# Attention and routed experts on one core: the third batch's table matmuls put behind the attention, the first slot's rows turned before the last value products, and conditional slots in groups of 4, 2 and 2

## The chip, the cores and the metric

The kernel runs on one core of a Trainium2 chip. The metric is the device time of one launch in microseconds (us). The profiled execution is a single launch with the hardware profiler on; its span is the time from its first to its last instruction.

## The reference

Four batches of 768 tokens with 8 heads of 64 are attended to in chunks of 32, each with 16 positions to its left, 8 to its right and 8 memory keys. The result, 3072 rows of 512, goes through a mixture of 8 experts of which each row takes one.

```python
for c in range(S // 32):
    k_full = concat(mem_k, k[c_start - 16 : c_end + 8])     # clipped to 0..S
    a = softmax(q_c @ k_full.T / sqrt(D))
    out[c] = a @ concat(mem_v, v[c_start - 16 : c_end + 8])
x = out.transpose(0, 2, 1, 3).reshape(3072, 512)
logits = x @ w_gate + modality_bias[modality_id]
e = argmax(logits); gate_w = softmax(logits)[e]
y[rows of e] = gate_w * (relu(x[rows of e] @ w1[e]) @ w2[e])
```

## The kernel before, in words

**Attention.** The work is cut into 32 units: 16 pairs of heads (four to a batch), each in two halves of the sequence. The main loop runs 34 times (`i` from 0 to 33, `n` is 32) and keeps three units in flight. For one unit `scores` (L356) makes the score products on TensorE, `exps_t` turns them (L374) and ScalarE takes their exponential (L376), `attend` makes the value products (L386), `normalize` divides on VectorE (L394 to L401) into a tile `xb`, and `trans_x` turns `xb` for the router (L409, copy L412) and, with the second half, stores it to `xd` in memory from GpSimd's queue (L414). In its last turns the loop finishes units 30 and 31, and the opening slot of the experts is begun.

**Routing.** After each batch a generator `route(b)` makes the logits (L546; ScalarE copies them in two halves, L549), turns them to token order (L556), finds each token's expert and rank on VectorE, makes one-hots of ranks and tokens (`l1`, L661, and `a1`, L663; for the third batch two of six tiles on GpSimd and the others on VectorE), and multiplies them in six matmuls (L671) to a table that says which token stands in which place. VectorE subtracts that into the table so far (L672). `pump` takes steps of the generator between pieces of the attention. A step that needs TensorE waits, "late" ones longer, until enough turns of the loop have passed; the table matmuls are such a late step. `B - 2` is the third batch, whose table comes in the last turns.

**Experts.** Tokens are gathered into slots of up to 256 rows of one expert. `gather` fetches a slot's rows from `xd` with two indirect DMAs on GpSimd's queue (L765) into the tiles `xg0` and `xg1`; the opening slot takes rows of the first batches alone, and its gather is issued in the turn `i` = 29. `trans(half)` turns them on TensorE (L804) and splits them into a high part (ScalarE, L780) and a low part (VectorE, L781). `load_w` loads an expert's weights on SyncE's queue (first weights L723 and L729, second L733), each into a `raw` tile; `conv` splits such a tile (ScalarE's cast L736; the rest on VectorE or GpSimd, L738). `mm1(f)` makes one eighth of the hidden layer in 12 matmuls (L822) with the relu on ScalarE (L823) and its low part on VectorE (L826); `mm2` makes the output (L832), which is scaled and scattered by an indirect DMA (L857).

**Slots.** After the opening slot and some fixed ones stand 8 short conditional slots (none is taken for these tokens; their branch line is L1131), two fixed slots, 8 conditional slots of the usual size (for these tokens four are taken; their branch line is L1137), and three last slots. Each group of conditions is nested: a slot's condition lies in the one before it, and all close together. An engine that finds a condition false jumps past the nested slots to a block that sets semaphores right for what was skipped, waits there for its own earlier work, and then branches behind the nest.

**What sets the order.** TensorE, SyncE and GpSimd run their instructions as written. ScalarE's and VectorE's are put in order by a scheduler from `i` = 26 on to the slots, and as written after that.

Of the kernel before, what the change touches and what calls it, by code (L numbers as in the profile page):

```python
# [21 lines left out]
B, H, S, D = 4, 8, 768, 64  # L22
# [33 lines left out]
def tile_chunk_attention_top1_moe(  # L56
# [39 lines left out]
    def bank():  # L96
        return ps.tile([P, 512], F32, name="tr", tag="tr", bufs=4)
# [210 lines left out]
    def regroup_q(u):  # L308
        q2 = q2s.pop(u)
        qr = qrs[u] = wk.tile([P, 6, 2, D], F32, name="qr", bufs=1)  # L310
        nc.vector.tensor_copy(
            qr.rearrange("p x h d -> p h x d"), q2.rearrange("p h (x d) -> p h x d", d=D)
        )
# [36 lines left out]
    def scores(u, hf):  # L350
        kbd, qT = kbds[u % 2], qTs[u]
        sc = scs[u, hf] = ps.tile([P, 512], F32, name="sc", tag="sc", bufs=2)
        for t in range(3):
            for j in range(4):
                c = 4 * (3 * hf + t) + j
                nc.tensor.matmul(  # L356
                    sc[32 * j:32 * j + 32, t * P:(t + 1) * P], qT[:, 32 * c:32 * c + 32],
                    kbd[:, c].rearrange("p h m -> p (h m)"), start=True, stop=True,
                )
# [9 lines left out]
    def exps_t(u, hf):  # L369

        sb = sbs.pop((u, hf)).rearrange("p a m -> p (a m)")
        t = bank()
        for i in range(3):
            nc.tensor.transpose(t[:, i * P:(i + 1) * P], sb[:, i * P:(i + 1) * P], ident)  # L374
        PT = PTs[u, hf] = wk.tile([P, 3 * P], F32, name="PT")
        nc.scalar.activation(PT, t[:, 0:384], AF.Exp, scale=scale)  # L376
# [14 lines left out]
    def normalize(u, hf):  # L391
        av = avs.pop((u, hf))[:, 0:3 * W].rearrange("p (t w) -> p t w", t=3)
        den = sm.tile([P, 3, 2, 1], F32, name="den")
        nc.vector.tensor_scalar(den[:, :, :, 0], av[:, :, 2 * D:W], 1e-9, None, op0=ALU.add)  # L394
        pump(1)
        nc.vector.reciprocal(den, den)
        pump(1)
        if hf == 0:
            xbs[u] = wk.tile([P, NT, P], F32, name="xb", bufs=3)
        dst = xbs[u].rearrange("p t (h d) -> p t h d", d=D)[:, 3 * hf:3 * hf + 3]  # L400
        nc.vector.tensor_mul(  # L401
            dst, av[:, :, 0:2 * D].rearrange("p t (h d) -> p t h d", h=2), den.to_broadcast([P, 3, 2, D]))

    def trans_x(u, hf):
        b, g = divmod(u, 4)
        xb = xbs[u]
        t = bank()
        for i in range(3):
            nc.tensor.transpose(t[:, i * P:(i + 1) * P], xb[:, 3 * hf + i, :], ident)  # L409
        if hf == 0:  # L410
            xTs[u] = rt.tile([P, S], F32, name="xT", bufs=5)
        nc.scalar.copy(xTs[u][:, 384 * hf:384 * hf + 384], t[:, 0:384])  # L412
        if hf == 1:
            nc.gpsimd.dma_start(xd[b * S:(b + 1) * S, g * P:(g + 1) * P].rearrange("(t p) c -> p t c", p=P), xb)  # L414


    routing, now = [], [0]

    def pump(k, pe=False):
        k *= KB if routing and routing[0][2] == B - 2 else 1  # L420
        while k > 0 and routing:
            g, wait, b, since = routing[0]
            if wait:
                if not pe or now[0] < since + (wait == "late" or b < B - 2) + (wait == "late" and b < B - 2):
                    return
                pe = False
            r = next(g, None)
            if r is None:
                routing.pop(0)
                return  # L430
            routing[0] = (g, r if r != "v" else "", b, now[0])
            k -= r == "v"
# [346 lines left out]
    def split(x, sl, cols):  # L779
        nc.scalar.copy(xth[:, sl, cols], x)  # L780
        nc.vector.tensor_sub(xtl[:, sl, cols], x, xth[:, sl, cols].bitcast(F32))  # L781
# [17 lines left out]
    def trans(half):  # L799
        t = bank().rearrange("p (c n) -> p c n", c=2)  # L800
        for cc in range(2):
            for tt in range(2):
                c = 2 * half + cc
                nc.tensor.transpose(t[:, cc, tt * P:(tt + 1) * P], xg[tt][:, c * P:(c + 1) * P], ident)  # L804
        split(t, slice(2 * half, 2 * half + 2), slice(0, 256))
# [8 lines left out]
    def mm1(f, rest=False, whole=True):  # L814
        w = 256 + (NR if rest else 0)
        pw = bank()[:, 0:w]
        ph = pw[:, 0:256]

        for n in range(12):
            wt, x, c = ((wh, xth), (wl, xth), (wh, xtl))[n // 4] + (n % 4,)  # L820
            i, j = (f, c) if whole else (f - f % 4 + c, f % 4)
            nc.tensor.matmul(pw, wt[i][:, j * P:(j + 1) * P], x[:, c, 0:w], start=(n == 0), stop=(n == 11))  # L822
        nc.scalar.activation(hh[:, f], ph, AF.Relu)  # L823
        if rest:
            nc.scalar.activation(hq[:, f], pw[:, 256:], AF.Relu)
        nc.vector.scalar_tensor_tensor(hl[:, f], ph, 0.0, hh[:, f].bitcast(F32), op0=ALU.max, op1=ALU.subtract)  # L826
# [88 lines left out]
    units = [(u, hf) for u in range(NU) for hf in range(2)]  # L915
    n = len(units)
    for i in range(n + 2):
        live = i < n
        u, hf = units[i] if live else (NU, i % 2)
        now[0] = i  # L920
        if i == MAN:
            man.close()
        if live and i < n - 1:
            scores(u, hf)
        if 1 <= i <= n:
            exps_t(*units[i - 1])
        if live:
            less_max(u, hf)
            pump(1)
        if u + 1 < NU and hf == 0:  # L930
            trans_k(u + 1)
            regroup_q(u + 1)
            pump(3)
            store_k(u + 1, 1, 0, nc.scalar.copy)
            store_k(u + 1, 0, 0, nc.scalar.copy)
            store_k(u + 1, 0, 1, nc.scalar.copy)
            store_k(u + 1, 1, 1, nc.scalar.copy)
            pump(3)
        elif u + 1 < NU:
            share_v(u + 1)  # L940
            if u + 2 < NU:
                mem_keys(u + 2, nc.gpsimd)
            trans_q(u + 1)
            store_q(u + 1, 0)
            store_q(u + 1, 1)
            pump(5)
        elif live:
            pump(5)
        if 2 <= i < n:
            trans_x(*units[i - 2])  # L950
        if i == n - 2:
            scores(*units[i + 1])
        if 1 <= i <= n:
            attend(*units[i - 1])
        if i == n:
            trans_x(*units[i - 2])
            trans(0)
            trans(1)
            conv(4)
            conv(5, nc.gpsimd)  # L960
            normalize(*units[i - 1])
            mm1(0)
        if i > n:
            mm1(1)
        if i > n:
            trans_x(*units[i - 2])
        if 1 <= i < n:
            normalize(*units[i - 1])
            pump(1)
        if i >= 2:  # L970
            u2, hf2 = units[i - 2]
            if hf2 == 1 and u2 % 4 == 3:
                routing.append((route(u2 // 4), True, u2 // 4, 0))
        if i == 1:
            routing.append((more_constants(), False, -1, 0))
        if i == 6:
            assert not routing
            bias_rows()
        if i < n:
            pump(1, True)  # L980
        if live and hf == 0:
            if 0 < u < NU - 3:
                load_qk(u + 3)
            if u >= 1 and u - 1 + NVW < NU:
                load_v(u - 1 + NVW)
            if u == NU - 3:
                load_w(0, 0)
        if (u, hf) == (NU - 2, 1):
            c_ld.close()
            xp = ctx.enter_context(tc.tile_pool(name="xp", bufs=1, side="right"))  # L990
            ix = xp.tile([P, 2], I32, name="ix")
            gx = xp.tile([P, 2], I32, name="gx")
            xg = [xp.tile([P, XW], F32, name=f"xg{t}", align_bytes=256) for t in range(2)]
            xth, xtl = [xp.tile([P, 4, 256 + NR], F32R, name=f"xt{i}") for i in range(2)]
            hh, hl = [xp.tile([P, 8, 256], F32R, name=f"h{i}") for i in range(2)]
            gather(0)
        elif u == NU - 1:
            conv(2 * hf)
            conv(2 * hf + 1, nc.gpsimd)
# [117 lines left out]
    more = ExitStack()  # L1117
# [14 lines left out]
    slot(ROW_R1, rest=0, rest_next=1)  # L1132
    slot(ROW_X, rest=1)
    for i in range(NEXTRA):
        more.enter_context(tc.If(nextra > i))
        slot(ROW_X + i + 1)
    more.close()  # L1137
# [32 lines left out]
```

## Time and profile before

| what | us |
|---|---|
| median of three runs | 445.32 |
| lowest and highest of them | 441.22, 449.06 |
| the profiled execution | 444.95 |
| span of the profiled execution | 442.9 |

The profiled execution's mean granted TensorE clock is 0.98 of full speed. In a timeline each row is a run of equal instructions: when it begins, how long it lasts, engine, source line, operation, result and operands by the program's names, the count, and in brackets the engine's idle time just before with what ended it. PE is TensorE, PEld its weight loads, DVE VectorE, ACT ScalarE, POOL GpSimd, SP SyncE; a small q marks an engine's instruction queue.

### The profile page before, as it was taken

How to read it: one execution, taken by the hardware profiler on the slowest of the kernel's cores; microseconds unless marked ns; L12 is line 12 of the kernel's file. 1: busy time of each engine (PE TensorE's matmuls, PEld its weight loads, DVE VectorE, ACT ScalarE, POOL GpSimd, SP SyncE). 2: the span in 40 equal slices, each digit the busy share in tenths (PEclk: the TensorE clock that was granted, in tenths of full speed). 3: DMA queues.
4: the chain of work that ended last, by engine and by line, in shares of the span. 5: the costliest groups of instructions: out<-in, count | busy, mean ns of one | idle time of the engine just before them, and what ended most of it. 6: DMA issues, size and time to landing. Idle time of an engine off the chain costs nothing. (4 is left out here: it accounts for less than half of the span.)

```text
span 442.9 us, 11892 instructions
## 1 busy us (share of the span) xinstructions
PE 416.2 (94%) x4053; PEld 356.6 (80%) x4053; DVE 309.7 (70%) x754; ACT 268.9 (61%) x537; POOL 204.6 (46%) x409
## 2 busy tenths in 40 slices
PE   7799999998978988999999999999999989999993
PEld 4677787877756968989798998989898969898982
DVE  7878697798687899848366356868686864959530
ACT  6857878786738555647366355656565654756521
POOL 7998879798496932450144205313131035020101
PEclk9989999999999998999999999999999998999998
DMA  6879988898756210487096967414795206140101
GB/s 200 218 195 276 253 211 242 224 246 214 187 139 220 83 34 22 123 268 189 28 274 210 202 218 262 123 73 123 154 262 223 72 15 204 33 142 1 48 1 48
DMA packets 78309, 69.33 MB, mean 157 GB/s; under 512 B 36763, under 2 KB 64563, under 8 KB 78228
## 3 DMA queue, kind: packets, MB, share of 16 engines
q1 hardware_dynamic: 71488, 48.84, 40.8%
q0 software_dynamic: 5888, 19.41, 14.2%
q8 instruction: 37, 0.61, 0.6%
q14 instruction: 44, 0.36, 0.3%
q10 hardware_dynamic: 852, 0.11, 0.2%
HBM read 81.25 MB, written 16.58 MB: 221 GB/s over the span
## 5 line engine op out<-in xcount | busy, mean ns | idle before, releaser
L822 PEld LDWEIGHTS tr<-xt,w 128*128 128x128 f32 x1152 | 142.3, 191 | 6.7 <-issue 4.0
L822 PE MATMUL tr<-xt,w 128*128 128x256 f32 (+1 forms) x1152 | 143.7, 286 | 3.9 <-issue 2.6
L832 PE MATMUL av<-wh,h 128*128 128x512 f32 x384 | 125.7, 399 | 0.0
L826 DVE SCALAR_TENSOR_TENSOR h<-tr,h 128x256 fp32r<-128x256 f32 x96 | 40.6, 424 | 66.2 <-ACT h L823 47.8
L832 PEld LDWEIGHTS av<-wh,h 128*128 128x128 f32 x384 | 72.4, 189 | 16.5 <-issue 0.4
L832 PE MATMUL av<-wl,h 128*128 128x512 f32 x192 | 75.8, 395 | 0.0
L823 ACT ACTIVATE h<-tr 128x256 fp32r<-128x256 f32 x96 | 36.7, 384 | 55.3 <-PE tr L822 45.6
L738 DVE TENSOR_TENSOR wl<-raw,wh 128x512 fp32r<-128x512 f32 x91 | 63.4, 698 | 8.7 <-ACT wh L736 1.6
L857 POOL DMA_INDIRECT out_dram<-o,ix x24 | 24.4, 1018 | 95.0 <-ACT o L853 92.8
L306 POOL COPY vw<-vw 24x384 f32<-24x384 f32 (+1 forms) x128 | 59.7, 504 | 10.0 <-DMA vw<-in_v_dram 8.5
L738 DVE TENSOR_TENSOR w<-raw,w 128x512 fp32r<-128x512 f32 x93 | 60.0, 685 | 5.1 <-ACT w L736 2.5
L736 ACT CAST wh<-raw 128x512 fp32r<-128x512 f32 x96 | 58.7, 615 | 0.0
L736 ACT CAST w<-raw 128x512 fp32r<-128x512 f32 x96 | 53.0, 621 | 0.1
L348 ACT COPY kbd<-tr 64x672 f32<-64x672 f32 x62 | 48.2, 777 | 4.6 <-PE tr L342 3.5
L832 PEld LDWEIGHTS av<-wl,h 128*128 128x128 f32 x192 | 36.3, 189 | 7.8
L853 ACT ACTIVATE o<-av,gate 128x512 f32<-128x512 f32 x24 | 16.3, 689 | 39.5 <-PE av L832 31.1
L765 POOL DMA_INDIRECT xg<-xd,gx x24 | 27.2, 1133 | 17.5 <-POOL gx L763 4.9
L376 ACT ACTIVATE PT<-tr 128x384 f32<-128x384 f32 x32 | 15.8, 493 | 29.5 <-PE tr L374 29.3
L386 PE MATMUL av<-vw,PT 128*32 128x130 f32 x768 | 29.4, 287 | 1.4 <-ACT PT L376 1.4
L356 PE MATMUL sc<-kbd,qT 128*32 128x128 f32 x768 | 27.6, 277 | 1.5 <-DVE kbd L348 1.3
L386 PEld LDWEIGHTS av<-vw,PT 128*32 128x32 f32 x768 | 20.2, 113 | 7.5 <-issue 3.8
L356 PEld LDWEIGHTS sc<-kbd,qT 128*32 128x32 f32 x768 | 20.7, 111 | 5.1 <-issue 3.4
(253 smaller groups left out, 519.1 us busy)
## 6 DMA issues: line engine op xcount, KB each, us to landing
raw<-in_moe_w_dram SPq DMA_DIRECT2D x192, 256.0 KB
k<-in_k_dram SPq DMA_DIRECT2D x16, 384.0 KB
q<-in_q_dram SPq DMA_DIRECT2D x16, 384.0 KB
xd<-xb POOLq DMA_DIRECT2D x16, 384.0 KB, 4.8
vw<-in_v_dram SPq DMA_DIRECT2D x32, 184.0 KB
xs<-xg SPq DMA_DIRECT2D x14, 256.0 KB
xq<-xs SPq DMA_DIRECT2D x28, 128.0 KB
vw<-in_mem_v_dram SPq DMA_DIRECT2D x32, 48.0 KB
```

Source lines behind the costliest of these rows:

```text
L306: nc.gpsimd.tensor_copy(vw[r0:r0 + 24, c + 1:c + 1 + w, d], vw[r0 + 32:r0 + 56, c:c + w, d])
L348: copy(dst.rearrange("p c (i j) -> p c i j", j=2)[:, :, :, j], win)
L356: nc.tensor.matmul(sc[32 * j:32 * j + 32, t * P:(t + 1) * P], qT[:, 32 * c:32 * c + 32], kbd[:, c].rearrange("p h m -> p (h m)"), start=Tr ...
L386: nc.tensor.matmul(avb[32 * j:32 * j + 32, t * W:(t + 1) * W], PT[:, t * P + 32 * j:t * P + 32 * j + 32], vw[:, c, 0:W], start=True, stop= ...
L736: nc.scalar.copy(wh[i], raw[i])
L738: (eng or nc.vector).tensor_sub(wl[i][:, s], raw[i][:, s], wh[i][:, s].bitcast(F32))
L765: nc.gpsimd.indirect_dma_start(out=xg[t], out_offset=None, in_=xd[0:rows], in_offset=bass.IndirectOffsetOnAxis(ap=at[:, t:t + 1], axis=0))
L822: nc.tensor.matmul(pw, wt[i][:, j * P:(j + 1) * P], x[:, c, 0:w], start=(n == 0), stop=(n == 11))
L823: nc.scalar.activation(hh[:, f], ph, AF.Relu)
L826: nc.vector.scalar_tensor_tensor(hl[:, f], ph, 0.0, hh[:, f].bitcast(F32), op0=ALU.max, op1=ALU.subtract)
L832: nc.tensor.matmul(pos[t], x, w[8 + f], start=(f == 0 and n == 0), stop=(f == 7 and n == 2))
L857: nc.gpsimd.indirect_dma_start(out=out, out_offset=bass.IndirectOffsetOnAxis(ap=to[:, t:t + 1], axis=0), in_=outs[t], in_offset=None, boun ...
```

## The change

Three edits. First, `pump` holds the late step of the third batch until the turn `i` = 32, where it is called for behind `mm1(0)`. Second, in that turn the gathered rows of the opening slot are turned first (`trans(0)`, `trans(1)`), then unit 30 (`trans_x`), and only then come the last value products (`attend`) and their normalization; in the turn after it `trans_x` stands ahead of `mm1(1)`. Third, the 8 conditional slots are closed behind the fourth and the sixth, so that they make three nests of 4, 2 and 2.

```diff
         if wait:
-            if not pe or now[0] < since + (wait == "late" or b < B - 2) + (wait == "late" and b < B - 2):
+            if not pe or (wait == "late" and b == B - 2 and now[0] < n) or now[0] < since + (wait == "late" or b < B - 2) + (wait == "late" and b < B - 2):
                 return
...
+        if i == n:
+            trans(0)
+            trans(1)
+            trans_x(*units[i - 2])
         if i == n - 2:
             scores(*units[i + 1])
         if 1 <= i <= n:
             attend(*units[i - 1])
         if i == n:
-            trans_x(*units[i - 2])
-            trans(0)
-            trans(1)
+            normalize(*units[i - 1])
             conv(4)
             conv(5, nc.gpsimd)
-            normalize(*units[i - 1])
             mm1(0)
-        if i > n:
-            mm1(1)
+            pump(99, True)
         if i > n:
             trans_x(*units[i - 2])
+            mm1(1)
...
     for i in range(NEXTRA):
+        if i in (4, 6):
+            more.close()
         more.enter_context(tc.If(nextra > i))
         slot(ROW_X + i + 1)
     more.close()
```

TensorE at the end of the attention, as the kernel before has it (the value products of unit 29 stand first; `tr` and `av` are results, `xg` the gathered rows, `xt` their split halves, `a1` and `l1` the one-hots):

```order
L386 MATMUL av_2781<-vw2_128,PT_2756 32x130 x12
L671 MATMUL tr_2798<-a1_2677,l1_2676 128x192
L671 MATMUL tr_2798<-a1_2681,l1_2680 128x192
L671 MATMUL tr_2798<-a1_2685,l1_2684 128x192
L671 MATMUL tr_2798<-a1_2689,l1_2688 128x192
L671 MATMUL tr_2798<-a1_2693,l1_2692 128x192
L671 MATMUL tr_2798<-a1_2697,l1_2696 128x192
L374 MATMUL tr_2816<-ident_144,sb_2760 128x128 x3
L409 MATMUL tr_2826<-ident_144,xb_2722 128x128 x3
L386 MATMUL av_2832<-vw0_126,PT_2820 32x130 x12
L374 MATMUL tr_2857<-ident_144,sb_2824 128x128 x3
L386 MATMUL av_2863<-vw0_126,PT_2861 32x130 x12
```

And the same stretch in the changed kernel, to the first of the gathered rows:

```order
L386 MATMUL av_2781<-vw2_128,PT_2756 32x130 x12
L374 MATMUL tr_2805<-ident_144,sb_2760 128x128 x3
L409 MATMUL tr_2815<-ident_144,xb_2722 128x128 x3
L386 MATMUL av_2821<-vw0_126,PT_2809 32x130 x12
L374 MATMUL tr_2846<-ident_144,sb_2813 128x128 x3
L804 MATMUL tr_2852<-ident_144,xg0_2731 128x128
L804 MATMUL tr_2852<-ident_144,xg1_2732 128x128
```

The six table matmuls are gone from here (they stand behind `mm1(0)` now), and the eight transposes of the gathered rows, which in the kernel before come behind the last value products and the turning of unit 30, stand ahead of both.

ScalarE's list around the two logit copies (L549), from the cast of the first of the second weights on, before:

```order
L736 CAST wh8_2952<-raw8_2951 128x512
L823 ACTIVATE h0_2735<-tr_2922 128x256
L736 CAST wh9_2955<-raw9_2954 128x512
L412 COPY xT_2880<-tr_2937 128x384
L549 COPY lgs_3003<-tr_3004 128x384
L736 CAST wh10_2958<-raw10_2957 128x512
L549 COPY lgs_3003<-tr_3010 128x384
L736 CAST wh11_2961<-raw11_2960 128x512
L736 CAST wh12_2964<-raw12_2963 128x512
```

And in the changed kernel:

```order
L736 CAST wh8_2952<-raw8_2951 128x512
L736 CAST wh9_2955<-raw9_2954 128x512
L412 COPY xT_2870<-tr_2922 128x384
L736 CAST wh10_2958<-raw10_2957 128x512
L736 CAST wh11_2961<-raw11_2960 128x512
L823 ACTIVATE h0_2735<-tr_2928 128x256
L736 CAST wh12_2964<-raw12_2963 128x512
L549 COPY lgs_3003<-tr_3004 128x384
L549 COPY lgs_3003<-tr_3010 128x384
```

Three more casts stand ahead of the first logit copy, and two more ahead of the second.

TensorE between the fourth and the fifth conditional slot, before:

```order
L832 MATMUL av<-wh_2973,h_2735 128x512
L832 MATMUL av<-wl_2974,h_2735 128x512
L832 MATMUL av<-wh_2973,h_2736 128x512
L1137 COMPARE_AND_BRANCH
L822 MATMUL tr<-xt_2733,w_192 128x256 x4
L822 MATMUL tr<-xt_2733,w_193 128x256 x4
L822 MATMUL tr<-xt_2734,w_192 128x256 x4
```

And in the changed kernel:

```order
L832 MATMUL av<-wh_2973,h_2735 128x512
L832 MATMUL av<-wl_2974,h_2735 128x512
L832 MATMUL av<-wh_2973,h_2736 128x512
L1137 UNCONDITIONAL_BRANCH x5
L1137 COMPARE_AND_BRANCH
L822 MATMUL tr<-xt_2733,w_192 128x256 x4
L822 MATMUL tr<-xt_2733,w_193 128x256 x4
L822 MATMUL tr<-xt_2734,w_192 128x256 x4
```

The compare stands where it stood; the branches of the first nest's end are new ahead of it, and the same with three branches stands behind the sixth slot. In the kernel before all nine branches of the nest stand behind the eighth slot.

## Rows read from the trace of the kernel before

**Rows 1.** The page, part 1: busy time, share of the span, instructions.

```profile
PE 416.2 (94%) x4053; PEld 356.6 (80%) x4053; DVE 309.7 (70%) x754; ACT 268.9 (61%) x537; POOL 204.6 (46%) x409
```

**Rows 2.** TensorE's timeline, 124 to 146 us (start, us, engine, line, operation).

```profile
127.75 0.36 PE L671 MATMUL tr<-a,l 128*128 128x192 f32 x1 [0.51 <-POOL a L663]
129.32 0.47 PE L671 MATMUL tr<-a,l 128*128 128x192 f32 x2 [1.22 <-POOL a L663]
130.23 1.32 PE L671 MATMUL tr<-a,l 128*128 128x192 f32 x3 [0.43 <-DVE a L663]
...
135.66 0.87 PE L386 MATMUL av<-vw,PT 128*32 128x130 f32 x24 [0.64 <-ACT PT L376]
136.47 0.55 PE L409 MATMUL tr<-ident,xb 128*128 128x128 f32 x3
136.85 1.07 PE L804 MATMUL tr<-ident,xg 128*128 128x128 f32 x8
138.59 3.33 PE L822 MATMUL tr<-xt,w 128*128 128x256 f32 x24 [0.67 <-ACT xt L780]
...
142.17 1.94 PE L546 MATMUL tr<-xT,wg 128*32 128x384 f32 x16
...
145.57 0.60 PE L556 MATMUL tr<-ident,lgs 128*128 128x128 f32 x4
```

**Rows 3.** GpSimd's timeline, 125 to 146 us.

```profile
128.27 1.00 POOL L663 TENSOR_SCALAR a<-iota,ac,tokm 128x192 fp32r<-128x192 f32 x1
...
130.42 1.18 POOL L765 DMA_INDIRECT xg<-xd,gx  x1 [0.30 <-issue]
131.90 0.98 POOL L765 DMA_INDIRECT xg<-xd,gx  x1 [0.30 <-issue]
```

**Rows 4.** The tile xg, 129 to 138 us (durations in ns; DMA landings).

```profile
L804 PE MATMUL tr<-ident,xg x8: 272/273/304, 136.8 to 137.6; 128*128 128x128 f32 x8
...
DMA to landing us min/median/max: 3.6/4.3/5.0
```

**Rows 5.** TensorE's timeline behind the first nest and behind the second.

```profile
220.05 1.17 PE L822 MATMUL tr<-xt,w 128*128 128x288 f32 x7 [0.66 <-PEq L1131]
...
363.35 0.40 PE L832 MATMUL av<-wh,h 128*128 128x512 f32 x1
366.33 2.04 PE L822 MATMUL tr<-xt,w 128*128 128x256 f32 x11 [2.58 <-issue]
```

**Rows 6.** Branch line L1137, whole span, then from 363.9 us (ns, min/median/max).

```profile
L1137 PEldq COMPARE_BRANCH  x6: 65/74/3446, 269.9 to 363.9; - x6
...
L1137 PEldq EVENT_SEMAPHORE  x1: 51/51/51, 363.8 to 363.8; - x1
...
L1137 PEldq COMPARE_BRANCH  x1: 2218/2218/2218, 363.9 to 363.9; - x1
```

**Rows 7.** TensorE's timeline, 157.5 to 169 us.

```profile
157.82 0.81 PE L671 MATMUL tr<-a,l 128*128 128x192 f32 x6
158.46 0.42 PE L832 MATMUL av<-wh,h 128*128 128x512 f32 x1
...
166.37 0.30 PE L804 MATMUL tr<-ident,xg 128*128 128x128 f32 x1 [2.17 <-DMA xg<-xd,gx]
```

**Rows 8.** Windows: us, busy PE, PEld, DVE, ACT, POOL, clock, DMA, GB/s.

```profile
131.60:135.00 3.40, 3.40 (x33) 2.15 (x31) 1.03 (x4) 1.49 (x3) 0.98 (x1) 0.50 0.70 193
135.00:138.40 3.40, 2.28 (x36) 1.77 (x35) 2.28 (x6) 2.87 (x6) 2.20 (x5) 1.00 0.14 29
```

**Rows 9.** Branch line L1131, whole span (ns, min/median/max).

```profile
L1131 PEldq COMPARE_BRANCH  x1: 3667/3667/3667, 216.1 to 216.1; - x1
```

**Rows 10.** SyncE's timeline, 134 to 142 us.

```profile
136.80 4.27 SPq L733 DMA_DIRECT2D raw<-in_moe_w_dram  x8
```

**Rows 11.** ScalarE's timeline, 141 to 146 us.

```profile
141.34 0.62 ACT L736 CAST wh<-raw 128x512 fp32r<-128x512 f32 x1
...
144.15 0.48 ACT L549 COPY lgs<-tr 128x384 f32<-128x384 f32 x1
```

## The prediction

> **What bounds the kernel now.** I read the page's busy shares first: TensorE is busy for 94% of the span, no other engine for more than 70% [rows 1]. A cut in the work of another engine is then worth nothing unless TensorE waits for it, and the change removes no matmul: it can only move waits of TensorE. So the next view was TensorE's timeline at the two places that the diff touches, and there the brackets, which name what ended each idle time.
>
> At the attention's end TensorE waits three times for one-hots of the third batch's table (0.51, 1.22 and 0.43 us), once for the exponentials of the last unit (0.64) and once for the first slot's turned rows (0.67): 3.47 us in all before the logits of the last batch begin at 142.17 [rows 2]. The POOL timeline tells why the one-hots are late: the last of them that POOL makes ends at 129.27, and behind it in the same queue stand a store and the two halves of the first slot's gather [rows 3]. The gathered rows take 3.6 to 5.0 us from issue to landing [rows 4].
>
> At the conditional slots, which for these tokens are taken four times of eight, TensorE stands 2.58 us between the last matmul of the fourth and the first of the slot behind the nest [rows 5]. The rows of the branch line there show one taken jump of 3446 ns that ended under matmuls still queued, the wait for the engine's own work at 363.8, and behind it a second jump of 2218 ns [rows 6].
>
> **The table held back.** It removes the waits of 0.51, 1.22 and 0.43 us [rows 2]: behind mm1(0) the one-hots have been ready for long. No matmul goes; the six take 0.64 us by their spacing in the fourth batch's table, which runs at the full clock [rows 7]. The table's own readers plan slots behind the opening one, so the 10 us of delay has cover: the next gather that TensorE waits for is the one before 166.37, and it hangs on the fourth batch's table, from 157.82 on [rows 7]. Its order stays as it was, so what shifts the head shifts it as much.
>
> **The rows turned earlier.** The transposes of the gathered rows now stand ahead of the last value products. Nothing in the change moves the gather: POOL's order is the same, and the one-hots that hold its queue are still made there. Its halves are issued at 130.42 and 131.90 [rows 3], so the second lands between 135.5 and 136.9 by the two ends of [rows 4]; I take the middle, 136.2. In before the transposes start at 136.85 without a wait, because TensorE comes that late [rows 2]. In after it is there at about 130 (three waits gone, some 2 us of value products and transposes put behind), and stands idle for some 6 us. The wait for the gather takes the place of the four that go. One queue is held meanwhile: behind the waiting transposes stand the turning of unit 30, the last value products and mm1(0); DVE's last normalization, the last store to xd and SP's loads of the second weights wait for the value products in their turn.
>
> What follows the landing, by spacings in [rows 2]: seven of the eight transposes at 0.114 us each (the busy 1.07 less 0.27 for the one in flight, over seven; 0.27 from [rows 4]) 0.80; unit 30's transposes 0.38; the value products 0.81; mm1(0) 1.60 (from 138.59 to 142.17, less 0.38 of transposes, over two); the table 0.64; the last transposes 0.38; mm1(1) 1.60. Sum 6.2 us. The copies that mm1(0) waits for in before (0.67) now lie beside unit 30 and the value products, 1.2 us, so I cost that wait at nothing; uncovered it is 0.7 at most. The clock adds something: after the waits of before the profile shows 3.40 us at a granted 0.50, and then 1.00 [rows 8]. A longer idle time in after should bring such a stretch too; if it lies wholly in the work after the landing it costs half its length, 1.7 us, if in the idle time nothing. I take half, 0.9. Logits: 136.2 + 6.2 + 0.9 = 143.3, against 142.17: **+1.1 us**. Low end 135.5 + 6.2 = 141.7, -0.5; high end 136.9 + 6.2 + 1.7 = 144.8, +2.6. From the logits on TensorE's order is that of before.
>
> **The groups.** Eight nested conditions become 4, 2 and 2. With four slots taken, one jump over four slots becomes two jumps over two. The first is hidden as now by the queued matmuls. At its landing the engine waits for its own work, as now (363.8), and only then comes the second jump, with nothing left to hide it. Its price: the two forward jumps that the trace shows took 3446 ns [rows 6] and 3667 ns [rows 9]; the 2218 ns that stands there now goes. That is +1.23 to +1.45, and 0.1 for one compare more (65 to 74 ns where not taken [rows 6]). I take **+1.4 us**, nearest to both rows. [...] From above: 3.67 and a short jump of 2.2 behind it as now, +3.7. No trace of before shows a jump over two slots.
>
> [...] The row shows 3446 ns for a jump over four slots, some 1150 instructions on TensorE (144 matmuls with as many weight loads in each) [rows 6]. [...]
>
> **Sum.** 444.95 (the profiled execution; span 442.9) + 1.1 + 1.4 = 447.5 us. That execution lies 0.4 under the median of the three runs, 445.32, whose spread is 441.22 to 449.06, so no correction.
>
> **Rivals.**
> First, faster: the jump over two slots is short. Its place is the end of the nest, its price -1.9, and it decides as soon as the second jump takes under about 1.1 us (the 2.2 that goes, less the head's +1.1). 444.95 + 1.1 - 1.9 = 444.2; with the head's low end 442.6. For it: half the distance of any jump shown. Against it: 3446 and 3667 ns, and nothing shorter that was taken. Chance 0.25.
> Second, slower: the second weights, not TensorE, end the head. SP issues their loads at 136.80, 0.27 after the last value products [rows 2, 10]; in after these end at about 138.2 to 139.2, the loads start up to 2.6 later (139.4). ACT's list now has five casts of these weights ahead of both logit copies, where before it had two ahead of the first and a third ahead of the second. First cast 141.34 + 2.6 = 143.9 [rows 11]; then up to the second copy five casts at 0.57, a 0.37 copy, a relu of 0.28 and the first logit copy 0.37 (spacings, estimates): 147.8 in place of 144.15, +3.7, less 0.94 that the transposes at 145.57 have in hand today [rows 2, 11]: +2.7 in place of +1.1, 449.1 us. It decides from an ACT lag over 2.0 us. For it: the order; against it: the casts may catch up if loads land fast. Chance 0.18.
> Third, the waits simply vanish: 3.5 off the head, 1.4 on, 442.9. It needs the gather in by about 132; [rows 3, 4] exclude it unless POOL comes earlier. Chance 0.04. A remainder of 0.03 goes to a slower tail, both jumps and a fetch, 451.
>
> **How the numbers follow.** The forecast has 0.50, its own range 445.5 to 449.5. Sums of the ends: 442.6 (-0.5 and -1.9) and 451.3 (+2.6 and +3.7). The range 441.7 to 451.8 adds about 0.7 for the executions' own spread. Within 2% is 436.4 to 454.2, about what a measurement of this kernel can tell from no change: every case lies in it. Faster 0.02, same 0.95, slower 0.03.
>
> **What would show it.** Right: TensorE's first idle row of some 4 to 6 us stands at the gathered rows' transposes, released by the gather near 136; no idle time at the table; logits near 143.3; two jumps of 3.4 to 3.7 us on the branch line and about 4.0 us of idle time ahead of the first last slot. Wrong: the transposes start before 134, the second jump is under 1 us, or the logits' copies come after 147.

## The result and the profile after

The changed kernel takes 450.37 us (median of 10 runs, 448.25 to 451.93) against 444.84 for the kernel before (10 runs): 1.0134 times as long, 95% interval 1.0104 to 1.0163, or 6.0 us with 4.6 to 7.3. The forecast was slower by 2.5 us. Its outer range (441.7 to 451.8) held the time, the forecast's own range (445.5 to 449.5) did not, and both of its terms were about half of what the profiles show.

The profiled execution took 451.93 us with a span of 450.1. The page's first part answers to [rows 1]:

```profile
PE 416.2 (92%) x4053; PEld 357.6 (79%) x4053; DVE 306.8 (68%) x754; ACT 268.8 (60%) x537; POOL 201.8 (45%) x409
```

TensorE's busy time is the same to the tenth. By this page what came is idle time alone, as forecast; the question is which.

TensorE's timeline at the attention's end, which answers to [rows 2, 7]:

```profile
127.72 0.85 PE L386 MATMUL av<-vw,PT 128*32 128x130 f32 x24
...
130.16 0.52 PE L409 MATMUL tr<-ident,xb 128*128 128x128 f32 x3 [1.11 <-DVE xb L401]
...
135.47 0.45 PE L804 MATMUL tr<-ident,xg 128*128 128x128 f32 x1 [3.52 <-DMA xg<-xd,gx]
136.89 1.76 PE L804 MATMUL tr<-ident,xg 128*128 128x128 f32 x7 [0.97 <-DMA xg<-xd,gx]
...
139.21 1.52 PE L386 MATMUL av<-vw,PT 128*32 128x130 f32 x24
140.67 1.89 PE L822 MATMUL tr<-xt,w 128*128 128x256 f32 x12
142.40 0.81 PE L671 MATMUL tr<-a,l 128*128 128x192 f32 x6
...
144.88 1.50 PE L546 MATMUL tr<-xT,wg 128*32 128x384 f32 x16
...
150.53 0.93 PE L556 MATMUL tr<-ident,lgs 128*128 128x128 f32 x6 [2.52 <-ACT lgs L549]
...
172.38 0.98 PE L804 MATMUL tr<-ident,xg 128*128 128x128 f32 x7 [1.15 <-DMA xg<-xd,gx]
```

The waits at the table (L671) are gone, and in their place stand 1.11 us for VectorE's normalization of unit 29, 4.49 at the gathered rows and, further on, 2.52 at the logits' transposes. The times can't be set beside those of before as they stand: at 103 us, ahead of everything that the change touches, the two executions already differ by 1.36 us, and the value products of unit 29 (127.72 above) begin 1.33 later than in the kernel before:

```profile
126.39 0.85 PE L386 MATMUL av<-vw,PT 128*32 128x130 f32 x24
```

Counted from these products, the logits begin at 17.16 in place of 15.78 us (+1.4) and their transposes at 22.81 in place of 19.18 (+3.6). That is against one execution: five further profiles with the old head (e1, e7, e9, e13 and e14 below) have the logits at 15.7 to 16.9 and the transposes at 19.1 to 20.3, and against the mean of all six the shifts are 1.0 and 3.3.

GpSimd's timeline (answers to [rows 3]), then SyncE's [rows 10] and ScalarE's [rows 11]:

```profile
131.77 1.18 POOL L765 DMA_INDIRECT xg<-xd,gx  x1 [0.30 <-PE av L386]
133.25 0.98 POOL L765 DMA_INDIRECT xg<-xd,gx  x1 [0.30 <-issue]
```

```profile
141.00 4.51 SPq L733 DMA_DIRECT2D raw<-in_moe_w_dram  x8
```

```profile
146.31 0.62 ACT L736 CAST wh<-raw 128x512 fp32r<-128x512 f32 x1 [1.02 <-DMA raw<-in_moe_w_dram]
147.75 0.62 ACT L736 CAST wh<-raw 128x512 fp32r<-128x512 f32 x1 [0.83 <-DMA raw<-in_moe_w_dram]
...
149.49 0.62 ACT L736 CAST wh<-raw 128x512 fp32r<-128x512 f32 x1 [0.83 <-DMA raw<-in_moe_w_dram]
150.01 0.85 ACT L549 COPY lgs<-tr 128x384 f32<-128x384 f32 x2
```

The gather is issued where it was (1.35 later, the shift of the execution). The second weights' loads begin 4.20 later, 2.87 by the clock of the value products, and ScalarE then waits for them three times with both logit copies queued behind.

The clock at the head (windows; the clock is the third number from the right), which answers to [rows 8]:

```profile
132.00:135.50 3.50, 0.03 (x1) 0.06 (x1) 2.58 (x8) 1.13 (x3) 3.19 (x5) 0.83 0.81 209
135.47:139.00 3.53, 2.56 (x11) 2.15 (x11) 0.51 (x1) 1.13 (x3) 1.56 (x3) 0.50 0.51 168
139.00:141.00 2.00, 2.00 (x27) 1.32 (x26) 0.35 (x3) 2.00 (x5) 1.73 (x5) 0.50 0.05 10
141.00:143.00 2.00, 2.00 (x18) 2.00 (x18) 2.00 (x5) 0.80 (x3) 2.00 (x4) 0.97 0.47 125
```

TensorE does nothing from 131.95 to 135.47. The clock falls within this idle time (0.83 over the first window) and stays at the lower level, a granted 0.50, to about 141: some 6.8 us by these windows, twice the 3.40 of before, and 4.2 of them lie behind the second landing at 136.89. Behind the wait of 2.52 us it falls once more, to 0.50 from 152.0 to 154.5.

At the conditional slots TensorE's timeline and the branch lines, which answer to [rows 5, 6] (the first false condition, that of the second nest, has the line L1137, that of the last nest L1140):

```profile
367.35 0.40 PE L832 MATMUL av<-wh,h 128*128 128x512 f32 x1
372.79 0.55 PE L822 MATMUL tr<-xt,w 128*128 128x256 f32 x1 [5.05 <-PEq L1140]
```

```profile
L1137 PEldq COMPARE_BRANCH  x6: 65/74/3732, 273.9 to 363.7; - x6
...
L1137 PEldq EVENT_SEMAPHORE  x1: 51/51/51, 367.8 to 367.8; - x1
```

```profile
L1140 PEldq COMPARE_BRANCH  x1: 4469/4469/4469, 368.0 to 368.0; - x1
```

The first jump (3732 ns) ends under the last matmul; the second, 4469 ns, begins at 368.0 with TensorE empty. Idle time 5.05 us in place of 2.58.

### The profile page after: what moved, and what is told of

The parts are those of the page before. It is cut to its first block, busy times and chain, and to the rows that moved or that the text cites. A ratio compares the mean times of both kernels' runs of the same rounds, so it can differ in the third digit from the quotient of the medians.

```text
span 450.1 us, 11917 instructions
## 1 busy us (share of the span) xinstructions
PE 416.2 (92%) x4053; PEld 357.6 (79%) x4053; DVE 306.8 (68%) x754; ACT 268.8 (60%) x537; POOL 201.8 (45%) x409
## 3 DMA queue, kind: packets, MB, share of 16 engines
q0 software_dynamic: 5888, 19.41, 13.8%
## 5 line engine op out<-in xcount | busy, mean ns | idle before, releaser
L822 PE MATMUL tr<-xt,w 128*128 128x256 f32 (+1 forms) x1152 | 145.4, 288 | 6.1 <-PEq L1140 5.0
L765 POOL DMA_INDIRECT xg<-xd,gx x24 | 27.2, 1132 | 16.9 <-POOL gx L763 4.9
```

Of the source, the lines that this page charges most:

```text
L765: nc.gpsimd.indirect_dma_start(out=xg[t], out_offset=None, in_=xd[0:rows], in_offset=bass.IndirectOffsetOnAxis(ap=at[:, t:t + 1], axis=0))
```

## The experiments

Each kernel ran in turn with the kernel before, in five rounds unless something else is said. A ratio is to that kernel before, with its 95% interval.

**The groups alone (e1).** The kernel before with

```diff
     for i in range(NEXTRA):
+        if i in (4, 6):
+            more.close()
```

> The kernel before with the groups of 4, 2 and 2 alone. Theory: the second jump stands uncovered behind the drain and takes what the changed kernel's row shows (4469 ns) in place of 2218, so TensorE's idle time ahead of the first last slot is 4.8 to 5.1 us in place of 2.58 and the time is 2.3 to 3.0 us over before (447.1 to 447.8). Rival: a jump costs 3.45 to 3.67 as in the forecast, the rest of the 4469 was this one execution; then +1.4 (446.2). Second rival: the whole loss of the change lies in the head; then +0.3 or less.

Measured: 448.3 us, ratio 1.0095 (1.0079 to 1.0111), 4.2 us. TensorE at the end of the nest:

```profile
366.93 9.35 PE L822 MATMUL tr<-xt,w 128*128 128x256 f32 x64 [4.44 <-PEq L1139]
```

The jump took 3934 ns, and the idle time is 1.9 us over before. The time lies above the theory's range: the groups are the larger part of the loss, and more than the one row explains. The profiled execution, 445.75 us, was the fastest of the seven runs.

**The same kernel, two more profiles (e13, e14; one execution each).**

> The kernel with the groups of 4, 2 and 2 alone, a second profile. Theory: the uncovered jump varies and was short in the first profile (3934 ns, idle time 4.44 us); here the idle time ahead of the first last slot is 5 to 7 us. Rival: the idle time is 4.2 to 4.8 us again, and what is missing lies elsewhere in the span.

> The same kernel, a third profile, with the same expectations: 5 to 7 us by the theory, 4.2 to 4.8 by the rival.

Measured: 448.48 and 448.6 us. The two idle times:

```profile
369.63 6.62 PE L822 MATMUL tr<-xt,w 128*128 128x256 f32 x41 [4.72 <-PEq L1139]
```

```profile
368.53 7.72 PE L822 MATMUL tr<-xt,w 128*128 128x256 f32 x40 [5.06 <-PEq L1139]
```

One on either side: the jump does vary (4214 and 4554 ns), but not enough for the rest. The three profiled executions of this kernel lie 1.4, 3.6 and 3.7 us over the median of the kernel before beside them, 2.9 in the mean. That is what the rows of the table below give (2.9), but three executions that far apart do not settle it against the timed 4.2.

**Groups of 4 and 4 (e7).** As e1 with `if i == 4:`.

> The kernel before with two groups of 4 and 4, so that for these tokens the first group is run whole and the second skipped by one jump over four slots. Theory that what costs is a jump behind the drain: there is one jump, still covered by queued matmuls, and behind the drain at most a short branch: TensorE's idle time ahead of the first last slot 0.6 to 2.6 us, the time equal to before or up to 2 us under it (442.9 to 444.9). Rival, each group's end costs something by itself (one more nest's end, whatever is jumped): 1 to 2 us over before.

Measured: 442.54 us, ratio 0.9955 (0.9938 to 0.9972), 2.0 us under before, the lower edge of the theory's range.

```profile
365.45 10.77 PE L822 MATMUL tr<-xt,w 128*128 128x256 f32 x89 [0.39 <-DVEq L1139]
```

One jump, covered, and behind the drain (the engine's wait for its own earlier work) nothing: the 2.58 us of before fall to 0.39. The granted clock stays at 1.00 as well. In before the windows at the join read

```profile
363.00:367.00 4.00, 1.43 (x10) 0.97 (x9) 0.00 (x0) 1.26 (x2) 3.04 (x3) 1.00 0.44 99
367.00:371.00 4.00, 4.00 (x24) 4.00 (x22) 1.12 (x2) 0.89 (x2) 1.01 (x1) 0.57 0.81 309
```

and with 4 and 4

```profile
363.00:367.00 4.00, 3.62 (x22) 2.90 (x22) 0.07 (x1) 1.27 (x2) 2.67 (x8) 1.00 0.17 28
367.00:371.00 4.00, 4.00 (x36) 4.00 (x36) 2.70 (x6) 2.68 (x6) 2.26 (x3) 1.00 0.78 270
```

so that 36 matmuls pass in four microseconds where there were 24. The second cost of a long idle time stands in these rows: the stretch at a lower granted clock behind it (0.57 over the window of before, 1.00 with 4 and 4). The end of a group costs nothing by itself; the rival fell. (The division fits these tokens: with a fifth slot taken the second group would be left from inside.)

**Groups of 4, 1, 1, 1, 1 (e8).** As e1 with `if i >= 4:`.

> The kernel before with groups of 4, 1, 1, 1 and 1: four taken jumps over one slot each, of which the first is covered and three stand behind a drain. Theory: a taken jump costs the same whatever it passes over, 3.4 to 4.5 us each: idle time ahead of the first last slot 10.5 to 13.8 us, the time 8 to 11 us over before (453 to 456). Rival: the price goes with the distance or falls away where the target is near (one slot is 288 instructions of TensorE): under 1.5 us each, 2 us over before or less (447 at most).

Measured: 452.53 us, ratio 1.0191 (1.0166 to 1.0216), 8.5 us over before. The branch rows and the idle time:

```profile
L1136 PEldq COMPARE_BRANCH  x2: 188/274/360, 359.3 to 359.6; - x2
```

```profile
L1136 PEldq COMPARE_BRANCH  x2: 414/1718/3022, 363.8 to 364.5; - x2
```

```profile
L1139 PEldq COMPARE_BRANCH  x1: 4917/4917/4917, 367.8 to 367.8; - x1
```

```profile
373.00 3.33 PE L822 MATMUL tr<-xt,w 128*128 128x256 f32 x14 [9.35 <-PEq L1139]
```

The theory's range held the time (8 to 11 us over), its idle time (10.5 to 13.8) did not come, so theory and rival were each half right. The four jumps over one slot each took 360, 414, 3022 and 4917 ns in order: over the same distance two were cheap and two cost 3 to 5 us. The cheap ones came after a run of plain code and after a wait of 3.8 us (359.96 to 363.8 by these rows); the dear ones right behind another jump, each some 0.3 us after its end.

**Groups of 4, 3 and 1 (e9).** As e1 with `if i in (4, 7):`.

> The kernel before with groups of 4, 3 and 1: the covered jump passes over three slots, the uncovered one over one slot, and the wait between them is short. [...] Rival: near targets are cheap whatever came before: under 0.6 us, idle time about 1 us, 1 to 2 us under before (442.8 to 443.8).

Measured: 447.69 us, ratio 1.0070 (1.0040 to 1.0101), 3.1 us over before.

```profile
L1139 PEldq COMPARE_BRANCH  x1: 3854/3854/3854, 364.7 to 364.7; - x1
```

```profile
368.87 7.38 PE L822 MATMUL tr<-xt,w 128*128 128x256 f32 x48 [4.36 <-PEq L1139]
```

A jump over a single slot, begun shortly after the jump over three had landed, cost 3854 ns. The rival, under 0.6 us for a near target, fell, and so did its 1 to 2 us under before: the distance alone does not set the price. No row shows what does.

**What the longer jumps share.** In the six profiles with one covered and one uncovered dear jump the second is always the longer, and it also falls where the DMA engines are at work. Beside each jump stands the mean busy share of the core's 16 DMA engines while it lasted.

| profile | slots passed over | first jump, ns (DMA share) | second jump, ns (DMA share) |
|---|---|---|---|
| changed kernel | 2, 2 | 3732 (0.05) | 4469 (0.50) |
| e1 | 2, 2 | 3372 (0.06) | 3934 (0.50) |
| e13 | 2, 2 | 3552 (0.05) | 4214 (0.51) |
| e14 | 2, 2 | 3512 (0.05) | 4554 (0.48) |
| e15 (below) | 2, 2 | 3412 (0.05) | 4254 (0.49) |
| e9 | 3, 1 | 3372 (0.05) | 3854 (0.51) |

Of e8's two dear jumps neither is covered and each stands right behind another; the windows of the third and the fourth (3022 and 4917 ns; the DMA share is the second number from the right):

```profile
364.50:367.52 3.02, 0.00 (x0) 0.00 (x0) 0.00 (x0) 0.00 (x0) 1.70 (x5) 0.90 0.04 8
367.80:372.72 4.92, 0.00 (x0) 0.00 (x0) 0.00 (x0) 0.00 (x0) 0.46 (x1) 0.50 0.53 162
```

In this pair the uncovered jump that met quiet DMA engines is as short as the covered ones above. So the rows go with the transfers and not with the cover, but it is one such pair, and no run moved the transfers away from a jump.

**The head edits alone (e2).** The changed kernel without the line pair of e1.

> The changed kernel without the groups (both head edits, one nest of 8). Theory: the head's loss is a chain: TensorE waits for the gathered rows, so the second weights' loads start 2.6 to 3 us later, so the logit copies, which stand behind five of their casts, come late, and TensorE waits 2.5 us at the logits' transposes; part of it comes back at the next gather: 2.2 to 2.8 us over before (447.0 to 447.6). Rival: only TensorE's own delay at the gather counts, +0.9 to +1.1 (445.9), and the rest of the difference was the spread of two executions.

Measured: 447.16 us, ratio 1.0057 (1.0031 to 1.0083), 2.5 us. Inside the theory's range. TensorE's rows differ in one point from the changed kernel's:

```profile
148.89 0.85 PE L556 MATMUL tr<-ident,lgs 128*128 128x128 f32 x6 [1.20 <-DVE h L826]
...
169.04 0.30 PE L804 MATMUL tr<-ident,xg 128*128 128x128 f32 x1 [0.67 <-DMA xg<-xd,gx]
170.52 1.58 PE L804 MATMUL tr<-ident,xg 128*128 128x128 f32 x7 [1.18 <-DMA xg<-xd,gx]
```

The wait at the logits' transposes is 1.20, and put down to VectorE; but ScalarE's logit copies are late here too (they begin at 148.09), and by an estimate from these rows the wait would be only some 0.3 us shorter without VectorE. The next gather's wait of 2.17 [rows 7] has shrunk to 0.67: there part of the loss comes back (how much is uncertain, for with the old head e1 and e13 wait 1.14 and 1.08 there).

**The table held back alone (e3).**

```diff
-            if not pe or now[0] < since + ...
+            if not pe or (wait == "late" and b == B - 2 and now[0] < n) or now[0] < since + ...
...
             mm1(0)
+            pump(99, True)
```

> The kernel before with the table matmuls held back alone; the gathered rows stay behind the last value products and unit 30. Theory: TensorE loses the waits for one-hots (2.2 us), gives about half back at the gathered rows, and the second weights start about 2 us earlier than before, so that their casts, which the list now puts ahead of the logit copies, do not come late: 0 to 1.2 us under before (443.6 to 444.8). Rival: the held table by itself is what costs (the scheduler's list with six casts ahead of the first logit copy): 1 to 2.5 us over before.

Measured: 443.73 us, ratio 0.9977 (0.9950 to 1.0005).

```profile
135.71 0.30 PE L804 MATMUL tr<-ident,xg 128*128 128x128 f32 x1 [1.94 <-DMA xg<-xd,gx]
136.29 0.98 PE L804 MATMUL tr<-ident,xg 128*128 128x128 f32 x7 [0.28 <-DMA xg<-xd,gx]
```

```profile
134.13 4.89 SPq L733 DMA_DIRECT2D raw<-in_moe_w_dram  x8
```

The gathered rows bring TensorE to a halt here too, but the last value products are behind it by then, and the weights' loads begin at 134.13, which is 7.1 us behind the value products of unit 29 (127.03 here), against 10.4 before and 13.3 in the changed kernel. The casts ahead of the logit copies do no harm: the logits' transposes begin at 146.55 without a wait. 1 us faster, with an interval that just reaches no change.

**The rows turned first alone (e4).** The order of the changed kernel's turn `i` = 32, without the held table and with one nest.

> The changed kernel's order with the gathered rows turned first, but the table matmuls at their old place and one nest of 8. Theory: TensorE waits 1 to 2 us at the gathered rows and the second weights start 1.5 to 2 us later than before, but the list has only two of their casts ahead of the logit copies: 0 to 1.2 us over before (444.8 to 446.0). Rival: turning the rows first is the whole of the head's loss: 2.2 to 2.8 over before (447.0 to 447.6).

Measured: 446.01 us, ratio 1.0024 (0.9995 to 1.0052), 1.1 us over before with an interval that reaches no change. That is the upper end of the theory's range. Its profiled execution has one VectorE instruction of 7.02 us (at 146.07) whose like take under 1, so its stages behind that are not read here. Ahead of it TensorE waits for one-hots as in before, and for the gathered rows only 0.45 us, less than the theory's 1 to 2. So neither head edit costs by itself what the two cost together: 1.1 us under before (e3) and 1.1 over (e4), neither clear of no change, against 2.5 over for both (e2). With the table at its old place its waits fill the time until the rows land.

**Logit copies ahead of the casts (e5).** The head edits with ScalarE's order written out:

```diff
     load_w(0, 1)
+    lgman = ExitStack()
+    lgman.enter_context(tc.manual_schedule(engines={mybir.EngineType.Activation}))
     conv(6)
...
     for f in range(3, 6):
+        for j in (2 * f + 2, 2 * f + 3):
+            conv(j, nc.gpsimd if j in CPOOL else None)
         mm1(f)
-    for f in range(8, 16):
+    for f in range(14, 16):
         conv(f, nc.gpsimd if f in CPOOL else None)
+    lgman.close()
```

> The head edits without the groups, and ScalarE's order written out from the second weights' loads on, so that both logit copies stand ahead of all casts of the second weights. Theory: the wait of 2.5 us at the logits' transposes falls to under 0.5 and the slow clock behind it goes: 1.5 to 2.7 us under the kernel with the head edits alone, that is within 0.7 of before (444.3 to 445.7). Rival: the wait only moves to the next gather or to the casts that now come later: the same time as with the head edits alone.

Measured: 447.36 us, ratio 1.0055 (1.0029 to 1.0082), the same as e2. The theory fell.

```profile
147.93 0.82 PE L556 MATMUL tr<-ident,lgs 128*128 128x128 f32 x6
...
169.60 0.30 PE L804 MATMUL tr<-ident,xg 128*128 128x128 f32 x1 [2.23 <-DMA xg<-xd,gx]
170.23 0.98 PE L804 MATMUL tr<-ident,xg 128*128 128x128 f32 x7 [0.33 <-DMA xg<-xd,gx]
```

The wait for the copies is gone, and the wait at the next gather, which had given time back, stands at 2.23 again. Even so TensorE is there only 0.7 us behind before, counted from the value products (128.09 here; 170.23 against 167.84), where e2 is 1.7 behind. The rest goes behind the gather: from 170.23 to the first slot behind the first nest e5 takes 52.8 us, the twelve other profiles that were measured so 51.2 to 52.2, and no row of waits tells why. The time did not follow when this wait was taken away.

**The gather issued earlier (e6).** The head edits, with the block that ends in `gather(0)` put into the same turn ahead of `pump(5)`, so that GpSimd issues it before the one-hots and the store instead of behind them.

> The head edits without the groups, and the first slot's gather issued ahead of GpSimd's one-hots and store instead of behind them. Theory: the rows land 3 to 4 us earlier, TensorE waits under 1.5 us for them (3.5 and 1.0 in the changed kernel), the second weights start at 137 or before by the clock of before, and the head gives 1 to 3 us back against before: 442 to 444. Rival: the gather is not what holds the head; the weights or the exponentials hold it: no better than before (444.8 or more).

Measured: 443.34 us, ratio 0.9969 (0.9947 to 0.9992), 1.4 us under before and 3.8 under e2, whose only difference is the place of the gather.

```profile
131.10 0.52 PE L409 MATMUL tr<-ident,xb 128*128 128x128 f32 x3 [2.51 <-DVE xb L401]
...
132.74 1.04 PE L804 MATMUL tr<-ident,xg 128*128 128x128 f32 x8
```

TensorE does not wait for the rows at all. What it waits for now is VectorE's normalization of unit 29.

**Head and groups together (e10, e11, e12).** First the changed kernel with groups of 4 and 4.

> The changed kernel with groups of 4 and 4 in place of 4, 2 and 2. Theory: the second uncovered jump is what the groups cost, and head and groups add up: the head's 2.5 us less the 2.0 that the groups of 4 and 4 gave alone: within 1 us of before (444.3 to 446.3). Rival: head and groups act on each other (a later head covers or uncovers other jumps): 447 or more.

Measured: 443.12 us, ratio 0.9953 (0.9927 to 0.9979). The same as e7 has without the head edits: in this pair the head cost nothing that shows, against 2.5 us between e2 and before, and 1.7 between the changed kernel and e1 (1.0134 less 1.0095). That is under the theory's range and further still from the rival's. The mean of the three pairs is 1.4 us for the head; they scatter by more than their intervals make likely. The mean granted clocks of the timed runs go the same way: 0.978 in e2 against 0.980 beside it, where the head cost 2.5 us, 0.976 against 0.977 where it cost 1.7, and 0.984 against 0.981 where it cost nothing. The kernel before shows the link in its own runs (442.16 us at 0.984 and 447.92 at 0.973 beside e15). So part of the scatter fits how long the lower clock lasted in each; what sets that was not tried.

Then e6 with groups of 4 and 4:

> The head edits with the gather issued ahead of GpSimd's one-hots, and groups of 4 and 4. Theory: the two gains add up, 1.4 and 2.0 us: 441.0 to 442.0 (ratio 0.990 to 0.995). Rival: TensorE's gain in the head is swallowed by the next gather or by the loads of the last slots: 442.5 or more, no better than the groups of 4 and 4 alone.

Measured: 440.03 us, ratio 0.9887 (0.9845 to 0.9929), 1 us under the theory's range: the groups of 4 and 4 gave 3.7 us over e6 in place of 2.0 (and 4.6 between e2 and e10).

And e3 with the early gather and groups of 4 and 4:

> The table held back, the gathered rows at their old place behind the last value products, the gather issued ahead of GpSimd's one-hots, and groups of 4 and 4. Theory: no wait for gathered rows, and the second weights' loads start as early as in the run with the table alone (some 3 us before those of before): the head gives 2 to 3 us, the groups 2.0: 440 to 441 (ratio 0.987 to 0.992). Rival: the wait for the second slot's gather swallows the head's gain: 442 to 443.

Measured: 439.05 us, ratio 0.9873 (0.9831 to 0.9915), 5.7 us under before, the fastest of all, again a little better than the theory's range, and faster than both kernels of the change.

```profile
133.46 1.53 PE L386 MATMUL av<-vw,PT 128*32 128x130 f32 x24 [0.64 <-ACT PT L376]
135.62 1.91 PE L804 MATMUL tr<-ident,xg 128*128 128x128 f32 x8
```

Here the last value products come first and the rows have landed when TensorE turns to them.

**That head with the other nests (e15 with 4, 2 and 2; e16 with one nest of 8).**

> The head with the table held back and the early gather, with groups of 4, 2 and 2. Theory: the groups cost the same under any head, 4.2 us over one nest of 8 and about 6 over the groups of 4 and 4 that gave 439.1: 444.5 to 446. Rival: under this head they cost what the rows at the nest say, 1.9 to 2.7 over one nest: 443 to 444.

> The same head with one nest of 8 as before. Theory: the groups of 4 and 4 gave 2.0 us of the 5.6 to 5.7, so this head gives 3.6: 441 to 442 (ratio 0.990 to 0.994). Rival: the head is worth what it was alone with the early gather, 1.4: 443 or more.

Measured: 446.57 us, ratio 1.0028 (1.0003 to 1.0054), and 443.15 us, ratio 0.9958 (0.9922 to 0.9993). So under this head the groups of 4, 2 and 2 cost 3.1 us over one nest (0.70%), and the groups of 4 and 4 give 3.8 (0.85%). e16 came out where its rival had it (443 or more). For e15 neither forecast of the time held: it came out a little over both, because e16 did; the step between the two lies between rows (1.9 to 2.7) and the first timing (4.2).

**Stages of the profiled executions**, worked out from start times on TensorE's timelines. Head: from the value products of unit 29 to the first slot behind the first nest. Idle: at the end of the second nest. Last slots: from there to the start of TensorE's last matmul. Tail: from that to the end of the span. All in us.

```
                    head   idle   last slots   tail
before              93.7   2.58   68.7         7.9
e1  (4, 2, 2)       92.7   4.44   68.7         8.3
e13 (the same)      93.0   4.72   68.7         8.3
e14 (the same)      92.7   5.06   69.9         8.3
e7  (4, 4)          93.3   0.39   67.1         8.3
e9  (4, 3, 1)       92.9   4.36   68.6         8.3
changed kernel      96.3   5.05   68.9         8.4
e2  (head, 8)       95.2   2.98   68.3         7.9
e5  (head, copies)  95.0   3.10   69.9         7.9
e10 (head, 4, 4)    95.0   0.43   67.2         8.3
e6  (head, gather)  91.2   2.38   68.6         7.9
e16 (8)             90.9   2.42   68.7         7.9
```

The stretch between the two nests is 143.7 us in every one of them. The head edits without the early gather cost 2.4 us (mean of the changed kernel, e2 and e10, 95.5, against 93.0 for before, e1, e13, e14, e7 and e9). The groups of 4, 2 and 2 cost 2.1 at the nest (mean 4.82 of the changed kernel, e1, e13, e14 and e15 with its 4.83, against 2.72 of six kernels with one nest: before, e2, e3 with 2.85, e5, e6 and e16), some 0.4 behind it and 0.4 in the tail: 2.9. Together 5.3, where 6.0 (4.6 to 7.3) was timed. The 69.9 of e14 and e5 among the last slots comes from the first 96 matmuls behind the nest, which take 14.2 us there (368.53 to 382.72 and 369.83 to 384.01) against 13.0 in e1 (366.93 to 379.91), where the mean granted clock is 0.57 from 367 to 371 and 1.00 after it. That the lower clock lasted longer in the two is an estimate from these spacings. By the same rows 4 and 4 are worth 3.3 us (2.2 at the nest and 1.5 behind it, less 0.4 in the tail), within the 2.0 to 4.6 of the four timed pairs.

## Why the prediction was wrong

**What bounds the kernel** stood: TensorE's busy time did not move, its waits did.

**The gather takes the place of the waits** was right, to the place and nearly to the size: 4.49 us and the 1.11 ahead of it, for the forecast's some 6. The rows landed at 136.89, by the clock of the value products 135.56 on the scale of before, the early end of the forecast's 135.5 to 136.9. e6 shows the mechanism by removing it: with the gather some 4 us earlier the head gives 3.8 us back.

**The clock term** was put at half of a stretch of 3.40 us, 0.9; from the second landing to the logits 8.0 us passed (136.89 to 144.88) in place of the 6.2 added up. The stretch lasted some 6.8 us and 4.2 of it lay behind the landing, which makes up to 2.1. The early landing and the longer stretch nearly cancel: logits +1.4 against the forecast's +1.1, or +1.0 against the six profiles with the old head. That this number came out is in part luck.

**"From the logits on TensorE's order is that of before"**, and so the shift stays as it is: this step failed. The shift grew to 2.3 to 3.6 us at the logits' transposes, where TensorE waited 2.52 us in the changed kernel and 1.40 in e10 for ScalarE's copies, the second rival's mechanism, and 1.20 in e2, ended by VectorE a little after the copies. The next gather's wait took part of it back. The prediction's own sign of being wrong came with it: the copies begin at 150.01, which is 148.7 on the scale of before, and it had said 147. What was left at the first nest is 2.4 by the rows and 0 to 2.5 by the timings, against 1.1. The second rival named the right rows and gave the head +2.7, but e5 shows that undoing its wait does not return the time, though it returns most of the shift as far as the next gather. What holds the head beyond the gather's own delay was not found.

**The groups' term, +1.4, was mis-sized most.** That the second jump stands uncovered was right, and so was the 2.2 us jump that goes. But the price was taken from the two covered jumps of before (3446 and 3667 ns). The five uncovered jumps over two slots that the profiles show took 3934 to 4554 ns, so that the nest lost 2.1. The distance is not why: the five covered jumps over two slots took 3372 to 3732 ns, like those of before over more. The long ones fell where the DMA engines were half busy; that the transfers lengthen them was not tried. The forecast charged nothing for the clock behind a longer idle time, nor for the tail, 0.8 together. 2.9 by the rows; 4.2 (3.5 to 4.9) by e1's timing, 3.1 by e15 against e16. The difference between the rows and e1's timing is open; the mean granted clock of e1's runs, 0.977, against 0.979 to 0.980 in the three profiles of that kernel, fits a part of it.

**The first rival**, a short jump over two slots, fell in each of the five profiles: the jumps over two slots took 3372 to 4554 ns, and only among those over one slot were there short ones (360 and 414 ns, beside 3022 to 4917). Its price of -1.9, which is also in the sum for the forecast's low end, stands for an idle time that falls from 2.58 us to the 0.66 that TensorE waits behind the first nest [rows 5]. No run shows that with a second jump over two slots: there the idle time rose to 4.44 to 5.06 us. It came to 0.66 or less only with the groups of 4 and 4, where no jump stands behind the drain: 0.39 in e7, 0.43 in e10, 0.52 in e11 and 0.34 in e12. No run shows either why some jumps over one slot are short and others are not.

## What to carry to other kernels

A taken jump of TensorE over one slot or more cost 3.0 to 4.9 us here, but for two of 0.4 us over a single slot, and it was free only while queued work covered it (3752 ns in e7, with 0.39 us of idle time behind them): count how many stand behind a drain before counting what they pass over. Before a consumer is moved ahead of other work, look at when its data is issued and land; moving the producer (here one gather ahead of four one-hots and a store on GpSimd) gave 3.8 us, more than the head edits had lost. And a wait that vanishes from one row is worth something only when the next wait on the same engine does not grow by it, as the one at the second gather did in e5.

## What was not expected

The short jump out of a nest of 8 (2.0 to 2.7 us in seven profiles) was worth more than its length: without it, in e7, the granted clock stays at 1.00 from 363 to 371 us (0.57 over 367 to 371 in before), and the last slots take 67.1 in place of 68.7 us. The tail behind the last matmul has two values, 7.9 us with one nest and 8.3 to 8.4 with most of the groups, though nothing in it was changed; its cause was not looked for.
